# Clustered attention and two MLPs in one program: the first gate weights and one output-weight tile converted inside the unwritten attention output, and another order at both ends of the first MLP

## The chip, the cores and the metric

The program runs on one core of one Trainium2 chip. The metric is the device time of one execution in microseconds (us). Five engines work side by side, each on its own queue in order: PE (matrix multiply; its weight loads are listed as PEld), DVE (vector), ACT (activation), POOL (GpSimd) and SP, which here only issues DMAs. "SPq" is such a queue's own time. A semaphore holds an instruction until what it needs is done, and everything behind it on that engine stands too.

## The reference, cut to what matters

```python
# attention: batch 2, 8 heads, 768 rows, head width 64, 16 clusters
q_assign, k_assign = argmax(normalised q . centroids), argmax(normalised k . centroids)
scores = where(q_assign == k_assign, q @ k.T / 8, -1e9)
x = softmax(scores) @ v                      # laid out as 1536 x 512
# first MLP, weights given as float64
x = sigmoid(x @ w_gate) * (x @ w_val) @ w_out          # 512 -> 1536 -> 512
# mixture of four experts
p = domain_probs / (domain_probs.sum(-1) + 1e-9)
out = sum over e of p[:, e] * (relu(x @ w1[e]) @ w2[e])   # 512 -> 1024 -> 512
```

## The kernel before, in words

**Numbers.** PE multiplies fp32 words of reduced width, so every operand is split into a high and a low part, and a product is three matmuls (high x high, high x low, low x high). A split is one ACT copy (the high part) and one subtraction on DVE or POOL (the low part). The weights of the first MLP arrive as 64-bit words. A *conversion* of 128x512 such words has six instructions: two ACT passes in `magnitude` (Abs of the upper word, line 628, and a scaled copy of the lower word in place, line 629), three DVE steps in `bits` (clamp, shift, sign: lines 634, 635, 636) and one integer add on POOL in `rounded` (line 641).

**Attention** is 96 steps: 8 pairs of heads (4 for each batch), 2 heads, 6 row blocks of 128. Step i issues the scores S of block i+2 (line 427) and their row maximum on DVE (line 430), a third of a value product PV (lines 460, 461), six transposes T of block i (line 447), their high part on ACT (line 450) and low part pl on DVE (line 451), and the exponential of block i+2 on ACT (line 438). The preparation of later pairs and the finishing of earlier ones are cut into named pieces. `SLOT` gives each piece a step, counted from its pair's first step, and a place in that step (0 before PV, 1 after it, 2 at the end). For instance, `q0` to `k1` transpose q and k and write hiq, loq, hik and lok; `rows0` and `rows1` copy these by DMA into the operands L and R of the two heads (lines 385 to 390); `mask0` and `mask1` copy the cluster codes (lines 396, 397); `spread`, `xadd` and `xscale` scale the finished output, which lies in self.X, one tile R0 or R1 of 4 x 768 words for each batch. A pair's quarter of the tile is written by its `xscale`. All of these DMAs go through SP's queue, in the order in which they are written. hik, like hiq, is one buffer: the next pair's hik waits until `rows1` has copied the one before.

**The tail.** From step 84 `TAIL` places the first MLP's opening: `open` gives the space of the attention's preparation to the MLP's pools; `load`, `mag`, `bits`, `round` load and convert the first unit of gate weights (00, 01 are its halves) and of value weights (10, 11), `sums` forms four sums of weight quarters on POOL (line 671), `split` splits them (lines 679, 680). The program-wide dummy Sigmoid of line 617 brings ACT's table of that function.

**First MLP** (`moe1`). A product of two 2x2-blocked matrices is made with seven block products instead of eight (`seven`, matmuls at line 761): four PSUM banks, adds on DVE (lines 774 to 796), and work of others taken from a list, one entry after the first product, one after each of the next adds. `gate` runs it for one batch and 256 gate columns and ends in Sigmoids (line 832); `value` multiplies by them on DVE (line 844) and splits the result G into high (ACT, line 845) and low (POOL, line 846); `outp` multiplies by two tiles of output weights (lines 646 to 648) and adds into an accumulator (line 867; ACT, line 865, in pass 0). Pass 0 is written out; passes 1 to 5 are a loop of gate(p,0), outp(p-1,1), value(p,0), gate(p,1), outp(p,0), value(p,1). Output tiles are loaded into one buffer, rwo: tile 1 of a pass can be loaded only when POOL's rounding of tile 0 has read it. Tile 0 is converted in outp(p-1,1), tile 1 in gate(p,1), split behind it.

**Seam and mixture.** In the last value and output blocks the batch-0 operands of the mixture are summed (`ys`, POOL, line 982) and split (`ysplit`, lines 978, 979), and the first expert weights converted; `moe2` then runs `hidden` (seven products) and `outp` for 32 groups.

Of the kernel before, what the change touches and what calls it, by code (L numbers as in the profile page):

```python
# [28 lines left out]
def r2(ap):  # L29
# [11 lines left out]
    "xadd": (17, 1), "xscale": (18, 0),  # L41
# [23 lines left out]

TAIL = {
# [9 lines left out]
class Net:  # L76
# [79 lines left out]
    def probs(self):  # L156
        nc, c = self.nc, self.cpool
        self.pn = c.tile([128, B, NT, E], F32, name="pn")
        for b in range(B):
            nc.scalar.dma_start(out=self.pn[:, b], in_=self.dp[b * S:(b + 1) * S].rearrange("(p t) e -> p t e", t=NT))  # L160
# [15 lines left out]
    def prep(self, n):  # L176
# [203 lines left out]
        def rows(hh):  # L380
            def go():
# [3 lines left out]
                dma(out=L1[0:64], in_=qh)  # L385
                dma(out=R1[0:64], in_=kh)
                dma(out=R1[64:128], in_=kh)
                dma(out=L1[64:128], in_=ql)
                dma(out=L2[0:64], in_=qh)
                dma(out=R2[0:64], in_=kl)  # L390
# [145 lines left out]
    def attention(self):  # L536
# [41 lines left out]
        self.u0 = [self.unit(0, which) for which in range(2)]  # L578
        self.outers = [self.outer(f) for f in range(F1 // 128)]
        tail = {"open": self.open_weights, "outer0": self.outers[0]["load"], "outer1": lambda: self.outers[1]["load"](True)}  # L580
        for which in range(2):
            u = self.u0[which]
            tail["sums%d" % which] = lambda u=u: u["sums"](pool)
            for a in range(2):
                for name in ("load", "mag", "bits", "round"):
                    tail["%s%d%d" % (name, which, a)] = lambda u=u, a=a, name=name: u[name](a)
            for k in range(4):
                tail["split%d%d" % (which, k)] = u["split"][k]
        for name, at in TAIL.items():
            work.setdefault((LAST + at[0], at[1]), []).append(tail[name])  # L590
# [24 lines left out]
        for _, g in pvs:  # L615
            list(g)
            self.nc.scalar.activation(self.warm1, self.half[:, 0:1], AF.Sigmoid)
# [7 lines left out]
    def magnitude(self, raw, f):  # L625

        lo_w, hi_w = self.words(raw)
        self.nc.scalar.activation(f, hi_w.bitcast(F32), AF.Abs, scale=float(2.0 ** 16))
        self.nc.scalar.activation(lo_w, lo_w.bitcast(U32), AF.Copy, scale=float(2.0 ** -29))
# [56 lines left out]
    def unit(self, p, which):  # L686
# [4 lines left out]
        def load(a):  # L691
            raws[a] = self.raw.tile([128, 2, 256], I64, name="raw", tag="raw")
# [6 lines left out]
        def mag(a):  # L699
            if a == 0:  # L700
                u["c"] = self.cv.tile([128, 2, 2, 256], F32, name="cv", tag="cv")
            self.magnitude(raws[a], half(a))
# [12 lines left out]
    def outer(self, f):  # L715
        nc, t = self.nc, {}

        def load(spare=False):
            t["r"] = self.raw.tile([128, 1, 512], I64, name="raw", tag="raw") if spare else \
                self.rwo.tile([128, 1, 512], I64, name="rwo", tag="rwo")  # L720
            nc.sync.dma_start(out=t["r"][:, 0, :], in_=self.wo[f * 128:f * 128 + 128, :])

        def mag():
            t["hi"], t["lo"] = (self.wom.tile([128, 512], F32R, name=n, tag=n) for n in ("woh", "wol"))
# [458 lines left out]
```

## Time and profile before

| what | value |
|---|---|
| median of 3 runs | 1086.05 us (1085.29 to 1087.23) |
| profiled execution, its own time | 1086.53 us |
| its span, first to last instruction | 1084.7 us |
| mean granted PE clock | 0.987 of full speed |
| busy: PE, PEld | 1041.2 us (96%), 966.0 us (89%) |
| busy: DVE, POOL, ACT | 824.4 us (76%), 637.5 us (59%), 548.5 us (51%) |

Attention ends near 278 us, the first MLP near 583 us; the rest is the mixture. A timeline row gives the start in us from the span's start, the duration, engine, line, operation, output<-inputs, shapes and count, and in brackets the idle time of the engine before it with what ended that. A row of stretches gives busy us of each engine (and instructions), the granted clock of PE, the share of time in which the 16 DMA engines were busy and GB/s. A group of waits gives us in total, times, longest.

### The profile page before, as it was taken

The numbers are of one execution on the slowest core, as the hardware profiler recorded it, in microseconds if no ns is written. First come the engines' busy times: TensorE is split into PE (matmuls) and PEld (weight loads), VectorE is DVE, ScalarE is ACT, GpSimd is POOL, SyncE is SP. The second block draws the span as 40 slices with busy tenths as digits, with TensorE's granted clock in tenths as the row PEclk, the third lists the DMA queues.
The fourth block names the chain that finished last, engine by engine and source line by source line (L and its number), as shares of the span: only waits on it lengthen the run. The fifth ranks groups of instructions, "written<-read, shape, count | busy, mean of one in ns | idle before, by whom it ended". The sixth has DMA issues, their size and how long they took to land.

```text
span 1084.7 us, 16243 instructions
## 1 busy us (share of the span) xinstructions
PE 1041.2 (96%) x5813; PEld 966.0 (89%) x5813; DVE 824.4 (76%) x1407; ACT 548.5 (51%) x1156; POOL 637.5 (59%) x568
## 2 busy tenths in 40 slices
PE   6999999997889999999998999999999999999998
PEld 5899999897789999999987899889988998899887
DVE  6999899899656677767767877777678867766765
ACT  4888799888555444444434433333334433333320
POOL 7566568776758666776777644444445544444430
PEclk8999999998989999999999999999999999999999
DMA  7667766753222111222120221222122312221201
GB/s 176 138 159 172 163 151 156 161 149 108 63 66 70 60 59 59 78 78 68 52 77 21 96 75 43 78 78 76 41 79 98 107 49 78 79 69 48 78 20 59
DMA packets 86480, 95.86 MB, mean 88 GB/s; under 512 B 42720, under 2 KB 59456, under 8 KB 86400
## 3 DMA queue, kind: packets, MB, share of 16 engines
q1 hardware_dynamic: 85968, 94.77, 32.1%
q8 instruction: 46, 0.75, 0.3%
q14 instruction: 34, 0.28, 0.1%
q10 hardware_dynamic: 432, 0.06, 0.0%
HBM read 65.07 MB, written 3.19 MB: 63 GB/s over the span
## 4 chain that ended last, share of the span: by engine, by line
PE 80%; DVE 9%; POOL 3%; ACT 3%; issue 2%; DMA 2%; SPq 0%; POOLq 0%; DVEq 0%; ACTq 0%
PE ph L761 31%; PE po L1058 8%; PE po L1059 8%; PE po L1057 8%; PE T L447 5%; PE S L427 4%; PE po L648 3%; PE po L647 3%; PE po L646 2%; PE PV L460 2%; PE PV L461 2%; DVE nm L430 1%; DVE pl L451 1%; DMA R<-hik 1%; POOL co L641 1%
## 5 line engine op out<-in xcount | busy, mean ns | idle before, releaser
L1014 POOL TENSOR_TENSOR wol<-r,woh 128x512 fp32r<-128x512 f32 x62 | 80.3, 1295 | 152.9 <-ACT woh L1013 151.7
L1064 DVE SCALAR_TENSOR_TENSOR acc<-po,pn,acc 128x512 f32<-128x512 f32 (+1 forms) x181 | 129.8, 742 | 36.3 <-PE po L1059 36.3
L1059 PE MATMUL po<-woh,h2l 128*128 128x512 f32 (+1 forms) x374 | 145.7, 389 | 0.0
L1058 PE MATMUL po<-wol,h2h 128*128 128x512 f32 (+1 forms) x374 | 145.6, 389 | 0.0
L1057 PE MATMUL po<-woh,h2h 128*128 128x512 f32 (+1 forms) x374 | 145.0, 388 | 0.0
L680 POOL TENSOR_TENSOR w1l<-sf,w1h 128x512 fp32r<-128x512 f32 x88 | 113.8, 1314 | 45.7 <-ACT w1h L679 42.7
L1033 ACT ACTIVATE h2h<-ph 128x384 fp32r<-128x384 f32 x128 | 62.6, 490 | 124.2 <-PE ph L761 96.9
L761 PE MATMUL ph<-h,w1h 128*128 128x384 f32 x336 | 114.2, 340 | 4.3 <-DVE ph L782 2.0
L761 PE MATMUL ph<-h,w1l 128*128 128x384 f32 x336 | 112.8, 336 | 0.7 <-POOL w1l L680 0.7
L761 PE MATMUL ph<-l,w1h 128*128 128x384 f32 x336 | 112.7, 335 | 0.0
L451 DVE TENSOR_TENSOR pl<-T,ph 128x384 fp32r<-128x384 f32 x192 | 97.3, 548 | 14.7 <-ACT ph L450 12.7
L679 ACT ACTIVATE w1h<-sf 128x512 fp32r<-128x512 f32 x88 | 55.7, 634 | 86.1 <-DVE sf L671 68.0
L1034 DVE SCALAR_TENSOR_TENSOR h2l<-ph,h2h 128x384 fp32r<-128x384 f32 x128 | 71.0, 554 | 34.0 <-ACT h2h L1033 30.8
L450 ACT ACTIVATE ph<-T 128x384 fp32r<-128x384 f32 x192 | 84.7, 493 | 21.0 <-PE T L447 20.5
L430 DVE TENSOR_REDUCE nm<-S 128x1 f32<-128x768 f32 x96 | 91.1, 949 | 2.0 <-PE S L427 1.0
L427 PE MATMUL S<-R,L 80*128 80x384 f32 (+1 forms) x384 | 91.4, 360 | 0.7 <-ACT P L438 0.7
L447 PE MATMUL T<-ident,P 128*128 128x128 f32 x576 | 83.3, 279 | 7.5 <-DVE pl L451 3.7
L438 ACT ACTIVATE P<-S,nm 128x768 f32<-128x768 f32 x96 | 87.7, 913 | 3.6 <-DVE nm L430 3.6
L680 POOL TENSOR_TENSOR w1l<-r,w1h 128x512 fp32r<-128x512 f32 x64 | 67.0, 1048 | 37.4 <-ACT w1h L679 37.4
L1059 PEld LDWEIGHTS po<-woh,h2l 128*128 128x128 f32 x374 | 70.2, 188 | 14.5
L1057 PEld LDWEIGHTS po<-woh,h2h 128*128 128x128 f32 x374 | 70.2, 188 | 13.9
L1058 PEld LDWEIGHTS po<-wol,h2h 128*128 128x128 f32 x374 | 70.2, 188 | 13.9
(264 smaller groups left out, 2851.7 us busy)
## 6 DMA issues: line engine op xcount, KB each, us to landing
r<-in_moe_w_dram SPq DMA_DIRECT2D x64, 512.0 KB, 3.6
L<-hiq SPq DMA_DIRECT2D x32, 192.0 KB, 4.6
R<-hik SPq DMA_DIRECT2D x32, 192.0 KB, 5.1
raw<-in_moe_w_gate_dram SPq DMA_DIRECT2D x12, 512.0 KB, 3.8
raw<-in_moe_w_val_dram SPq DMA_DIRECT2D x12, 512.0 KB, 3.8
rwo<-in_moe_w_out_dram SPq DMA_DIRECT2D x11, 512.0 KB, 3.5
nq<-in_q_dram SPq DMA_DIRECT2D x16, 192.0 KB, 4.5
nk<-in_k_dram SPq DMA_DIRECT2D x16, 192.0 KB, 3.6
```

What stands on the lines that cost most here:

```text
L427: nc.tensor.matmul(ps[:, a, 0:384], l[0:k, c], r[0:k, a * 384:a * 384 + 384], start=l is L1, stop=l is L2)
L430: nc.vector.tensor_reduce(nm, ps[:, :, 0:384], axis=AX.XY, op=ALU.max, negate=True)
L438: nc.scalar.activation(r2(pt), ps[:, :, 0:384], AF.Exp, bias=nm, scale=1.0, accum_out=P["sums"][:, i:i + 1])
L447: nc.tensor.transpose(ps[:, j, :], pt[:, c:c + 128], self.ident)
L450: nc.scalar.activation(hi, ps, AF.Copy)
L451: nc.vector.tensor_tensor(lo, ps, hi.bitcast(F32), op=ALU.subtract)
L680: nc.gpsimd.tensor_tensor(lo[:, sl], x, hi[:, sl].bitcast(F32), op=ALU.subtract)
L761: nc.tensor.matmul(ps, x[:, a, j], y[:, j], start=first and j == 0 and k == 0, stop=j == 1 and k == 2, skip_group_check=not first)
L1057: nc.tensor.matmul(ps, Hh[:, f, c], wh[:, dc], start=f == 0, stop=False)
L1058: nc.tensor.matmul(ps, Hh[:, f, c], wl[:, dc], start=False, stop=False)
L1059: nc.tensor.matmul(ps, Hl[:, f, c], wh[:, dc], start=False, stop=f == 1)
L1064: nc.vector.scalar_tensor_tensor(a, ps, pe, a, op0=ALU.mult, op1=ALU.add)
```

## The change

The first unit of gate weights and output tile 0 are converted in steps 12 to 52 (`SOON`) inside self.X, in parts that no pair has written yet; the tail keeps the value unit's conversion, earlier and spread over steps, and the splits of the gate unit move to steps 85 and 86. `t1`, the first operand sum of batch 1, is put at step 86, and the table load at step 93. `rows1` comes half a step earlier, with the key rows first for the second head; `xadd` and `xscale` half a step later. The domain probabilities are loaded by SP's queue instead of ACT's and normalised in value(0,1). In `moe1` the conversion of output tile 1 moves to the first gate block in pass 0 and into value(p,0) in the loop; at the end the operand splits and the conversion of pair 1 get another order. `spare1`, `temp1` and `room` are the former inner functions of `moe1`.

```diff
 SLOT
-"rows1": (-7, 0)   "xadd": (17, 1), "xscale": (18, 0)
+"rows1": (-8, 1)   "xadd": (18, 0), "xscale": (18, 2)
+SOON = {
+    "load00": (12, 2), "load01": (13, 2), "abs00": (15, 2), "low00": (24, 2), "bits00": (24, 25, 27), "round00": (28, 2),
+    "abs01": (27, 2), "low01": (36, 2), "bits01": (36, 37, 39), "round01": (40, 2),
+    "loado": (29, 2), "abso": (39, 2), "lowo": (48, 2), "bitso": (48, 49, 51), "roundo": (52, 2),
+}
 TAIL = {
-    "open": (-12, 0), "load00": (-12, 0), "load01": (-12, 0),
-    "mag00": (-10, 2), "bits00": (-9, 1), "round00": (-9, 1), "load10": (-9, 1),
-    "mag01": (-9, 2), "bits01": (-8, 1), "round01": (-8, 1), "load11": (-8, 1), "sums0": (-7, 2),
-    "split00": (-7, 2), "split01": (-6, 2), "mag10": (-5, 2), "split02": (-5, 2), "bits10": (-4, 1), "round10": (-4, 1),
-    "split03": (-4, 2), "outer1": (-4, 2), "mag11": (-4, 2), "bits11": (-3, 1), "round11": (-3, 1), "outer0": (-6, 2),
-    "sums1": (-2, 2),
+    "open": (-12, 0), "load10": (-12, 0), "load11": (-12, 0), "sums0": (-12, 2), "outer1": (-11, 2),
+    "split00": (-11, 2), "split01": (-11, 2), "split02": (-10, 2), "split03": (-10, 2), "t1": (-10, 2),
+    "mag10": (-9, 2), "bits10": (-8, -8, -7), "round10": (-7, 2), "mag11": (-7, 2), "bits11": (-6, -6, -5),
+    "round11": (-5, 2), "sums1": (-3, 2), "table": (-3, 2),
 }
 def probs
-            nc.scalar.dma_start(out=self.pn[:, b], ...
+            nc.sync.dma_start(out=self.pn[:, b], ...
+    def normalise(self):
 def rows
+                parts = [(L1[0:64], qh), (R1[0:64], kh), (R1[64:128], kh), (L1[64:128], ql), (L2[0:64], qh),
+                         (R2[0:64], kl)]
+                for o, x in [parts[i] for i in ((0, 1, 2, 3, 4, 5) if hh == 0 or first else (1, 2, 0, 4, 5, 3))]:
+                    dma(out=o, in_=x)
 def attention
-        self.u0 = [self.unit(0, which) for which in range(2)]
+        R0, R1 = (x.rearrange("p a s -> p (a s)") for x in self.X)
+        raws = [r.bitcast(I64)... for r in (R1[:, 0:1024], R0[:, 2048:3072])]
+        self.u0 = [self.unit(0, 0, raws, R1[:, 1536:2560]...), self.unit(0, 1)]
+        o0 = self.outer(0, raws[0], R1[:, 2560:3072])
...
         for _, g in pvs:
             list(g)
-            self.nc.scalar.activation(self.warm1, self.half[:, 0:1], AF.Sigmoid)
 def moe1
-        c, d = conv(o0), conv(o1)
-        sums["t1"]()
+        d = conv(o1)
-        gate(0, 0, [[lambda: split0(6, Q), vs[0]], [lambda: split0(2, V), vs[1]], c[0] + [vs[2]], c[1] + [vs[3]],
-                    c[2], c[3] + c[4], [xadd, xscale, o0["split"]]])
+        gate(0, 0, [[lambda: split0(6, Q), vs[0]], [lambda: split0(2, V), vs[1]], [vs[2]] + d[0], d[1] + [vs[3]],
+                    d[2], d[3] + d[4] + [o0["split"]], [xadd, xscale]])
-        value(0, 0, [[sums["t2"]], [go[0]] + d[0], d[1] + [sums["t3"]], d[2], d[3] + d[4], [sums["t4"], o1["split"]],
-                     [lambda: split(0, V), go[1]]])
+        value(0, 0, [[o1["split"], go[0]], [sums["t2"]], [go[1]], [], [], [], [sums["t3"], lambda: split(0, V), sums["t4"]]])
-        value(0, 1, [load(U[1][1])] + [[go] for go in U[1][0]["split"]])
+        value(0, 1, [load(U[1][1])] + [[go] for go in U[1][0]["split"]] + [[self.normalise]])
             o1["load"]()
-            value(p, 0, [[], [o0["split"]]])
             e = conv(o1)
+            value(p, 0, [[], [o0["split"]], [], e[0], e[1], e[2], e[3] + e[4]])
-                gate(p, 1, [e[0], e[1], e[2], e[3] + e[4], [o1["split"]] + c[0], c[1] + c[2], c[3] + c[4]])
+                gate(p, 1, [[o1["split"]], c[0], c[1], c[2], c[3], c[4]])
-        gate(NP - 1, 1, [e[0], e[1], e[2], e[3] + e[4], [o1["split"]]])
+        gate(NP - 1, 1, [[o1["split"]]])
-        value(NP - 1, 1, [[ys[0], out[1], lambda: self.load_out2(1)], [lambda: ysplit(0, V), ys[1]], [lambda: ysplit(1, V)], []])
-        outp(NP - 1, 1, [[ys[2], lambda: ysplit(4, V)], [ys[3]], [lambda: ysplit(5, V)], [lambda: ysplit(3, V)],
-                         [lambda: ysplit(6, Q)], [], [lambda: ysplit(2, Q)], [cin[0], cin[1]]], soon=True)
-        self.first_in = cin[2:]
+        value(NP - 1, 1, [[ys[0], out[1], lambda: self.load_out2(1)], [lambda: ysplit(0, V), ys[1]], [ys[2]], [], [], [],
+                          [cin[0], lambda: ysplit(4, V)]])
+        outp(NP - 1, 1, [[ys[3], lambda: ysplit(5, V)], [cin[1]], [lambda: ysplit(3, V)], [cin[2]],
+                         [lambda: ysplit(1, V)], [cin[3]], [lambda: ysplit(6, Q)], [lambda: ysplit(2, V), cin[4]]], soon=True)
+        self.first_in = []
```

In `unit` and `outer` a place that is given is used for the raw words and the result instead of a tile of the pools; `mag` can issue its two ACT passes apart; output tile 1 of pass 0 is loaded into rwo instead of a buffer of raw; the high and low tiles of an output tile are taken in `split` instead of in `mag`.

## Rows read from the trace of the kernel before

**Rows 1.** Stretches: start:end, length, busy us of each engine, PE clock, DMA share.
```profile
88.30:122.30 34.00, 31.95 (x209) 29.97 (x207) 30.06 (x53) 26.84 (x65) 23.58 (x20) 0.95 0.64 147
241.70:278.40 36.70, 31.27 (x177) 28.43 (x176) 30.00 (x48) 29.37 (x67) 23.55 (x21) 0.86 0.43 121
278.40:313.10 34.70, 27.48 (x129) 24.92 (x128) 23.76 (x29) 19.57 (x38) 24.20 (x17) 0.90 0.15 46
393.85:441.55 47.70, 46.82 (x266) 45.60 (x265) 35.04 (x64) 21.63 (x42) 33.42 (x33) 1.00 0.21 67
```

**Rows 2.** Timeline of PE in the attention tail (steps 85, 86, 93 and 95).
```profile
243.76 0.81 PE L447 MATMUL T<-ident,P 128*128 128x128 f32 x6
245.82 0.82 PE L447 MATMUL T<-ident,P 128*128 128x128 f32 x6
...
266.70 0.90 PE L447 MATMUL T<-ident,P 128*128 128x128 f32 x3 [3.44 <-ACT ph L450]
...
272.27 1.48 PE L447 MATMUL T<-ident,P 128*128 128x128 f32 x6
```

**Rows 3.** Source lines of the conversion: count, ns min/median/max, first and last start.
```profile
L634 DVE TENSOR_SCALAR cv<-cv x24: 414/890/1295, 248.7 to 527.0; 128x512 f32<-128x512 f32 x24
...
L635 DVE TENSOR_SCALAR cv<-cv x24: 414/427/1419, 249.2 to 527.4; 128x512 int32<-128x512 int32 x24
...
L636 DVE SCALAR_TENSOR_TENSOR cv<-raw,cv x24: 678/682/1649, 249.6 to 529.2; 128x512 int32<-128x512 int32 x24
...
L628 ACT ACTIVATE cv<-raw x24: 649/670/738, 248.0 to 524.7; 128x512 f32<-128x512 f32 x24
```

**Rows 4.** Timeline of ACT behind the last transposes.
```profile
276.11 1.28 ACT L617 ACT_TABLE_LOAD   x1
277.40 0.20 ACT L617 ACTIVATE warm<-half 128x1 f32<-128x1 f32 x1
```

**Rows 5.** Waits of PE in the MLP's start: us, times, longest.
```profile
PE po L647 <- POOL G L846: 2.8, 2, 2.0
```

**Rows 6.** Timeline of DVE, PE and ACT in the middle of attention.
```profile
107.47 0.20 DVE L163 TENSOR_REDUCE pns<-pn 128x12 f32<-128x48 f32 x1 [0.45 <-DMA pn<-in_moe_domain_probs_dram]
...
111.16 1.36 PE L447 MATMUL T<-ident,P 128*128 128x128 f32 x6 [1.80 <-DVE pl L451]
...
199.41 0.49 ACT L259 ACTIVATE hik<-T 128x384 fp32r<-128x384 f32 x1 [1.78 <-DMA R<-hik]
...
74.15 0.49 ACT L259 ACTIVATE hik<-T 128x384 fp32r<-128x384 f32 x1 [0.67 <-DMA R<-hik]
```

**Rows 7.** Stretches in the middle of attention, columns as in rows 1.
```profile
66.00:76.00 10.00, 9.54 (x67) 8.82 (x66) 8.75 (x17) 7.27 (x18) 4.37 (x3) 1.00 0.94 214
111.70:115.00 3.30, 3.30 (x13) 3.21 (x13) 3.08 (x5) 2.16 (x6) 2.91 (x6) 0.50 0.31 75
```

**Rows 8.** Timeline of PE and POOL in loop pass 2 (output product; rounding of tile 0).
```profile
410.58 0.44 PE L648 MATMUL po<-G,wol 128*128 128x384 f32 x1 [0.75 <-POOL wol L737]
...
396.53 1.32 POOL L641 TENSOR_TENSOR co<-co,rwo 128x512 int32<-128x512 int32 x1 [0.63 <-DVE co L636]
```

**Rows 9.** Tile rwo: its loads from issue to landing.
```profile
DMA to landing us min/median/max: 3.4/3.5/3.5
```

**Rows 10.** Chain of waits where a value block meets the gate block: start, us, what.
```profile
401.17 0.56 DVE ph L796
401.73 0.47 DVE sg L844
...
402.24 1.32 PE ph L761 x6
```

**Rows 11.** Waits of PE at the seam to the mixture: us, times, longest.
```profile
PE ph L761 <- DVE ph L782: 2.7, 2, 1.5
...
PE ph L761 <- POOL w1l L680: 0.7, 1, 0.7
```

**Rows 12.** Timeline of DVE at the seam.
```profile
566.67 2.13 DVE L979 TENSOR_TENSOR Y<-acc,Y 128x768 fp32r<-128x768 f32 x1
```

More of the change, by code (lines that the diff above doesn't have):

```diff
@@ L584, in attention @@
             for a in range(2):
-                for name in ("load", "mag", "bits", "round"):
+                for name in ("load", "mag", "round"):
                     tail["%s%d%d" % (name, which, a)] = lambda u=u, a=a, name=name: u[name](a)
+                tail["bits%d%d" % (which, a)] = lambda steps, u=u, a=a: u["bits"](a, steps)
             for k in range(4):
                 tail["split%d%d" % (which, k)] = u["split"][k]
-        for name, at in TAIL.items():
-            work.setdefault((LAST + at[0], at[1]), []).append(tail[name])
+        for names, gos, base in ((SOON, soon, 0), (TAIL, tail, LAST)):
+            for name, at in names.items():
+                if name[:4] == "bits":
+                    for k in range(3):
+                        work.setdefault((base + at[k], 1), []).append(lambda go=gos[name], k=k: go((k,)))
+                else:
+                    work.setdefault((base + at[0], at[1]), []).append(gos[name])
         def side(i, pos):
@@ L684, in left_operands, with unit @@
                    split(slice(5, 7), lambda: t["sf"][:, 2:4]), split(2, lambda: t["r"][:, 1, :, 128:256])]
-    def unit(self, p, which):
+    def unit(self, p, which, place=None, result=None):
         src = (self.wg, self.wv)[which]
@@ L691, in load @@
         def load(a):
-            raws[a] = self.raw.tile([128, 2, 256], I64, name="raw", tag="raw")
+            raws[a] = place[a] if place else self.raw.tile([128, 2, 256], I64, name="raw", tag="raw")
             self.nc.sync.dma_start(out=raws[a], in_=src[a * 256:a * 256 + 256, p * 256:p * 256 + 256]
@@ L697, in half, with mag @@
             return u["c"][:, a].rearrange("p k f -> p (k f)")
[L699 to L702, printed above, removed]
+        def mag(a, steps=(0, 1)):
+            if "c" not in u:
+                u["c"] = result if place else self.cv.tile([128, 2, 2, 256], F32, name="cv", tag="cv")
+            self.magnitude(raws[a], half(a), steps)
         def bits(a, steps=range(3)):
@@ L713, in unit, with outer, load, mag @@
         return u
-    def outer(self, f):
+    def outer(self, f, place=None, result=None):
         nc, t = self.nc, {}
-        def load(spare=False):
-            t["r"] = self.raw.tile([128, 1, 512], I64, name="raw", tag="raw") if spare else \
-                self.rwo.tile([128, 1, 512], I64, name="rwo", tag="rwo")
+        def load():
+            t["r"] = self.rwo.tile([128, 1, 512], I64, name="rwo", tag="rwo") if place is None else \
+                place.rearrange("p k f -> p (k f)").unsqueeze(1)
             nc.sync.dma_start(out=t["r"][:, 0, :], in_=self.wo[f * 128:f * 128 + 128, :])
-        def mag():
-            t["hi"], t["lo"] = (self.wom.tile([128, 512], F32R, name=n, tag=n) for n in ("woh", "wol"))
-            t["f"] = self.co.tile([128, 512], F32, name="co", tag="co")
-            self.magnitude(t["r"], t["f"])
+        def mag(steps=(0, 1)):
+            if "f" not in t:
+                t["f"] = self.co.tile([128, 512], F32, name="co", tag="co") if place is None else result
+            self.magnitude(t["r"], t["f"], steps)
         def bits(steps=range(3)):
@@ L735, in split @@
         def split():
+            t["hi"], t["lo"] = (self.wom.tile([128, 512], F32R, name=n, tag=n) for n in ("woh", "wol"))
             nc.scalar.activation(t["hi"], t["f"], AF.Copy)
@@ L807, in moe1 @@
         gs, sgs = {}, {}
-        def room(pool, t, dt=F32R):
-            return pool.tile([128, 2, HB], dt, name=t, tag=t)
-        def spare(o):
-            if o == 2:
-                return room(self.xsp, "rb"), room(self.xp, "tA")
-            if o == 6:
-                return room(self.xsp, "A"), room(self.xsp, "W")
-            return room(self.op, "g%d" % o), room(self.op, "k%d" % o)
-        def temp(o):
-            return room(self.cv, "cv", F32) if o > 4 else room(self.xp, "tA" if o == 4 else "tB", F32)
-        sums, split = self.right_operands(1, spare, temp, nc.gpsimd)
+        room = self.room
+        sums, split = self.late
         split0 = self.split0[1]
```

46 lines of the change are left out of this document (33 added, 13 removed), and 2 rows, old and new, of the table SLOT.

## The prediction

> **What bounds the kernel now.** On the page PE is the busiest engine in nearly every slice, so time can only come from stretches where it stands or runs at its lower clock. A table of stretches shows where: a pass of the first MLP's loop has PE busy 46.82 of 47.70 us at full clock, the last twelve steps of attention 31.27 of 36.70 and the first blocks of the MLP 27.48 of 34.70, at 0.86 and 0.90 of the clock [rows 1]. At the lower level (1.2 of 2.4 GHz) a microsecond does half the work, so the attention tail lost 5.4 us standing and 36.7 x 0.14 = 5.1 to the clock, the MLP's start 7.2 and 3.5. After that I read the timeline, the waits and the chain of waits inside each stretch [rows 2 to 12]: the reader is to see which instruction ended each hole.
>
> **The attention tail.** A step is 2.06 us from transposes to transposes where nothing stands, as the first two of [rows 2] show; the next nine take 26.45 us, 7.9 too many. The largest hole is 3.44 us. It ends on ACT's copy of T, but behind it stands DVE with a conversion: one half of 512 words is three DVE instructions of 0.41, 0.41 and 0.68 us alone, and 1.29, 1.42 and 1.65 at their longest (1.5 against 4.4 us a half) [rows 3], the long ones while POOL runs. The change takes two halves of four out of the tail. Two remain, beside POOL's splits, so they may cost 4.4 each. ACT loses two halves of 2 x 0.67 [rows 3] and gains the table load, 1.28 us and its dummy of 0.20 [rows 4], which stood where ACT was idle and now stands ahead of the last copies of T. The splits of the gate weights come earlier, together with POOL's four sums; ACT waits for those sums, with the copies of T queued behind. Bounds: 9 us gained (the hole, its clock and half a microsecond) to 2 (both halves at the long price, the clock falls anyway). I take **6**: the halves no longer stand behind one another, but ACT is fuller at steps 85 to 89.
>
> For the table load there is a rule. Here the load took 1.28 us and the next ACT instruction began 0.01 us after it [rows 4]. The Trainium skill, "ScalarE: Activation LUTs", section "What ACT_TABLE_LOAD costs", states a load plus a drain, about 2.66 us together; by that the tail would gain 1.2 us less. The trace shows no such drain here.
>
> **The MLP's start.** PE waits 2.8 us for POOL's low halves of G [rows 5], while POOL rounds and splits tile 1 of the output weights among them. After the change tile 0 comes converted and tile 1 takes its place in the first gate block: that block has the same DVE and POOL work as now, but the value block loses a round and its three DVE steps (1.5 to 4.4 us [rows 3]). The new wait: DVE's xscale writes over tile 0's result, so it stands until POOL has split that, with the value block's adds behind it on DVE. POOL comes to that split about when it does now, so I count 1 us. Bounds: 3 (the wait for G alone) to 10.7 (all that this stretch lost). I take **7**.
>
> **The middle of attention.** Gains: the four small DVE steps on the domain probabilities begin at 107.47, ahead of a row maximum; PE then stands 1.80 us [rows 6] and runs 3.3 us at the lower clock [rows 7], 1.8 + 1.65 = 3.45. They move to the end of the value block of pass 0, where DVE has room [rows 1]. Copying the key rows first lets ACT overwrite hik one copy earlier: ten copies of 192 KB fill a 10 us stretch at a DMA share of 0.94 [rows 7], 0.94 us each, off a wait of 1.78 us [rows 6]; I count 0.9. The half step by which rows1 moves passes nothing on SP's queue: 0.
>
> Costs: two 512 KB loads now stand on SP's queue at steps 12 and 13, ahead of the attention copies and rows1 of that round, in the stretch just named, which is full. A loop pass holds six such loads at a share of 0.21 of 47.70 us [rows 1], 1.67 us each. So key rows land 3.3 - 0.94 = 2.4 us later, and ACT, which already waits 0.67 us for them there [rows 6], waits 3.1; behind it stand U and the next PV. With the lower clock after it (1.65) that is 4.0. Bounds: 0, if the loads pass beside the copies, to 6. I take 4.0, since copies in this stretch are late already. Nine DVE steps join three pairs: 4.6 us cheap to 13 dear, against 3.9 us free in 34 by the first of [rows 1], in steps where POOL mostly idles. 0 to 5; I take 1.5. ACT's six passes (0.67 each, 7.2 of 34 us free) and POOL's three rounds (1.3 each, 10.4 free) I cost at nothing; without that room each would cost its own length once. The same goes for xadd and xscale half a step later, the third load at step 29 and the probabilities' two issues on SP, all of which stand after rows1. Sum: 3.45 + 0.9 - 4.0 - 1.5 = **-1.2**.
>
> **The loop.** In each of five passes the output product waits 0.75 us for POOL's split of tile 1, and restarts slowly (0.44 us for that one product) [rows 8]: 1.0 together. Its conversion now comes in the value block, and that loss goes: 5 x 1.0 = 5. But its load waits for the one buffer, which POOL's rounding of tile 0 frees at 397.85 [rows 8]; it lands 3.4 us on [rows 9], at 401.3, just where the value block's products end (401.14). The conversion is written after the first eviction, so ACT stands for the load, then 0.67 us of Abs; DVE's first bit step (0.4) stands until then, and the two adds and the eviction that free the bank for the next gate block's second product stand behind it, with the second bit step (0.4) between. Today that chain is add 0.56, multiply 0.47, PE, with no slack [rows 10]. New: 401.3 + 0.7 + 0.4 + 0.5 + 0.4 + 0.5 + 0.5 = 404.3 instead of 402.2, a hole of 2.1 us, or 3.2 if the second bit step meets POOL (1.42). Net 5 x 2.1 - 5 = 5.5, to 11; if nobody is held it is the gain of 5. I take **-6**, near the cheap end, as POOL is idle when the first step runs.
>
> **The seam to the mixture.** PE waits 2.7 us in two holes for one add on DVE and 0.7 for the weights of pair 1 [rows 11]. A split of 2.13 us stands ahead of that add on DVE [rows 12] and leaves; pair 1's sums and splits move ahead of the seam. In exchange POOL has three sums instead of two ahead of G, so the wait for G may grow by one sum, 1.9 us. Bounds 0 to 4.5 (the two waits and the slow restarts behind them); I take **3**.
>
> **Sum**: 6 + 7 - 1.2 - 6 + 3 = 8.8 us. The profiled execution took 1086.53 us around a span of 1084.7; it stands 0.5 above the median of 1086.05. 1086.5 - 8.8 = 1077.7, in terms of the median **1077**. What this kernel can tell from no change is 0.2%, 2.2 us.
>
> **Rivals.**
> 1. *Both ends gain and the loop pays part back* (forecast, 0.46): 1077, with 1071 to 1084 of its own.
> 2. *The loop gains too* (0.17): the late conversion holds nobody, because it doesn't stand where the diff writes it or its load lands 2 us sooner. For it: POOL's rounding that frees the buffer waits on DVE steps that meet POOL today, and could come sooner; against: in the loop of the kernel before, DVE's order is the written one. 5 instead of -6: 1066.
> 3. *Slower* (0.21): the hole of the loop is at its long end, 3.2 us, and the lower clock follows each one. For it: holes of 1.80 and 3.44 us idle [rows 2, 6] were followed by it [rows 1, 7]; against: 2.1 us is nearer to the shorter of them, and each pass alike would have to meet POOL. 5 x (3.2 + 1.65 - 1.0) = 19 lost instead of 6: 1090. It decides from a net loss of 3.4 us a pass, where the other 14.8 us are used up by 2.2 more.
> 4. *The loss only moves* (0.16): in the middle the nine DVE steps meet POOL at the long price (-3.5 more), and the tail, full on ACT, gains 2 instead of 6: 1085, no change.
>
> **Chances.** Faster: all of 2, nearly all of 1 and little of 4, 0.65. Within 0.2%: most of 4 and a rest of 1 and 3, 0.14. Slower: most of 3, some of 4, 0.21. The range goes from rival 2 with its tail near the upper bound, 1064, to rival 3, 1090.
>
> **What the profile after would show.** Right: no hole over 2 us between steps 86 and 95 and no lower clock there; the wait of the output product for G under 1 us; no DVE work on pn in attention; a wait of ACT for R<-hik near 3 us at step 18; in each pass a new hole of 2 to 3 us at the gate's second product ended by DVE's multiply, and none for wol. Wrong: no such hole (rival 2), the lower clock in every pass (rival 3), or holes at steps 24 to 52 that end on DVE's pl (rival 4).

## The result, and the profile after

The changed kernel took **1097.06 us** (median of 4 runs, 1092.86 to 1100.0) against 1085.67 for the kernel before: ratio 1.0100, 95% interval 1.0062 to 1.0138. It is slower by 1%, where 0.8% faster was forecast. The profiled execution (1095.45 us) has a span of 1093.7 us against 1084.7, so 9.0 us are to be found. One of the twelve executions of start_order (run 8 below) took 2062.55 us where the others took 1079.9 to 1086.0; its ratio leaves that one out.

The page of the changed kernel, span, busiest engines and granted clock:

```profile
span 1093.7 us, 16218 instructions
...
PE 1043.5 (95%) x5813; PEld 971.4 (89%) x5813; DVE 821.6 (75%) x1408; ACT 549.1 (50%) x1155; POOL 638.9 (58%) x567
...
PEclk8999999999999999999999999999999999999999
```

Little there tells that 9 us were lost: PE has 2.3 us more busy time and 6.7 us more idle time. Stretches tell more. In the next view the first row is the attention tail, from step 84 to attention's last product, where the forecast cut it too [rows 1]; the second and third are the MLP's start, up to gate(0,1) and up to the loop; then come two loop passes, the second and the third, each from one first product of `outp(p,0)` to the next (columns as in [rows 1]):

```profile
243.20:279.90 36.70, 31.25 (x186) 28.09 (x184) 28.55 (x43) 27.34 (x63) 21.87 (x20) 0.95 0.27 82
279.90:311.70 31.80, 25.93 (x119) 22.54 (x118) 21.59 (x26) 18.01 (x34) 22.42 (x16) 0.89 0.12 39
311.70:345.50 33.80, 31.02 (x176) 30.09 (x175) 23.15 (x38) 20.86 (x44) 24.71 (x24) 1.00 0.22 63
363.60:413.90 50.30, 48.04 (x265) 47.19 (x264) 34.38 (x63) 21.76 (x42) 33.73 (x33) 0.97 0.21 63
413.90:464.20 50.30, 46.57 (x265) 45.62 (x265) 34.41 (x63) 21.76 (x42) 33.77 (x32) 1.00 0.21 63
```

Cut at the same instructions, the kernel before gives the lengths of the second column:

| stretch | before | after | gain | forecast |
|---|---|---|---|---|
| start of attention to its step 84 | 241.7 | 243.2 | -1.5 | -1.2 |
| step 84 to attention's last product | 36.7 | 36.7 | 0.0 | +6 |
| MLP's start, from there to gate(0,1) | 34.6 | 31.8 | +2.8 | +7 |
| gate(0,1) to value(1,0) | 33.0 | 33.8 | -0.8 | 0 |
| loop, value(1,0) to value(5,1) | 215.4 | 227.3 | -11.8 | -6 |
| value(5,1) to the end | 523.3 | 520.9 | +2.3 | +3 |

The sum is -9.0. (Of the first row 1.0 us lies ahead of attention's second step, where the changed code is the same; other profiles have -0.2 to +0.9 there. loop_only, run 2 below, has the attention of the kernel before and reaches step 84 0.9 us later than it, so a difference of 1 us in this row says little.) The MLP's first products stand between attention's last ones, 14 matmuls of them ahead of attention's last product where 5 stood before, so the second and third rows run into each other; their sum, 2.8 of 13, is firmer than either. A loop pass is 50.3 us instead of 47.7 [rows 1]. Where PE stood, by what ended it (engine, line waited for: us in total, times, longest):

```profile
PE ph L788 <- DVE sg L872: 11.3, 6, 2.2
PE T L452 <- DVE pl L456: 8.4, 6, 2.7
PE ph L788 <- DVE ph L809: 5.6, 5, 1.5
...
PE po L673 <- POOL G L874: 3.2, 2, 2.5
...
PE ph L788 <- DVE u L801: 2.6, 1, 2.6
```

L872 is the multiply of `value` (L844 before), and five of its six waits are the loop's. The wait for `wol` [rows 8] is gone. But L809, the add of `gate`, is new in the loop: 4.4 of the 5.6 us lie in passes 1, 3 and 4. The timeline of pass 2, POOL, ACT, DVE and PE in order of time, and last a row of pass 3:

```profile
397.92 1.31 POOL L667 TENSOR_TENSOR co<-co,rwo 128x512 int32<-128x512 int32 x1 [0.63 <-DVE co L662]
...
402.90 0.66 ACT L653 ACTIVATE co<-rwo 128x512 f32<-128x512 f32 x1 [1.13 <-POOL G L874]
...
403.60 0.43 DVE L660 TENSOR_SCALAR co<-co 128x512 f32<-128x512 f32 x1 [1.93 <-ACT co L653]
403.94 0.56 DVE L818 TENSOR_TENSOR ph<-u,ph 128x384 f32<-128x384 f32 x1
404.40 0.42 DVE L661 TENSOR_SCALAR co<-co 128x512 int32<-128x512 int32 x1
404.74 0.55 DVE L823 TENSOR_TENSOR ph<-u,ph 128x384 f32<-128x384 f32 x1
405.20 1.01 DVE L872 TENSOR_TENSOR sg<-sg,ph 128x384 f32<-128x384 f32 x2
...
405.81 0.44 PE L788 MATMUL ph<-g,w1h 128*128 128x384 f32 x1 [2.20 <-DVE sg L872]
...
410.64 1.29 POOL L764 TENSOR_TENSOR wol<-co,woh 128x512 fp32r<-128x512 f32 x1 [0.74 <-ACT woh L763]
...
411.15 1.07 DVE L660 TENSOR_SCALAR cv<-cv 128x512 f32<-128x512 f32 x1 [1.37 <-ACT cv L653]
412.14 0.55 DVE L809 TENSOR_TENSOR ph<-u,ph 128x384 f32<-128x384 f32 x1
...
463.08 0.44 PE L788 MATMUL ph<-rb,w1h 128*128 128x384 f32 x1 [1.50 <-DVE ph L809]
```

The upper part is the forecast's chain, step for step: POOL's rounding ends at 399.23 and frees the one buffer, the load is issued at 399.25, ACT's Abs starts at 402.90, one of DVE's steps stands ahead of the first add (L818) and one between the two, PE stands 2.20 us (forecast 2.1). In the five passes the hole is 1.42, 2.20, 2.16, 1.99 and 2.04 us. The row of the Abs names POOL's G, which ended at the same moment, but Abs doesn't read G; in the other four passes, where it starts 3.4 to 3.6 us behind the issue, the row names the load. The lower part wasn't forecast: the first step of the *gate* conversion (L660 on `cv`) begins while POOL splits tile 1, takes 1.07 us instead of 0.43, and the add L809 stands behind it. In pass 2 PE doesn't wait for that add, as it ran at half clock between 406.8 and 409.9 us and came later; in pass 3, at full clock, the same order makes it stand 1.50 us.

The attention tail, DVE and POOL:

```profile
254.19 2.14 DVE L660 TENSOR_SCALAR cv<-cv 128x512 f32<-128x512 f32 x1
254.22 1.83 POOL L525 TENSOR_TENSOR tB<-R 128x768 f32<-128x768 f32 x1
...
260.69 1.82 POOL L507 TENSOR_TENSOR A<-A,W 128x768 f32<-128x768 f32 x1
...
260.90 1.90 DVE L660 TENSOR_SCALAR cv<-cv 128x512 f32<-128x512 f32 x1
262.59 1.87 POOL L510 TENSOR_TENSOR R<-A,rb 128x768 f32<-128x768 f32 x1
...
262.83 1.91 DVE L661 TENSOR_SCALAR cv<-cv 128x512 int32<-128x512 int32 x1
...
265.26 0.55 PE L452 MATMUL T<-ident,P 128*128 128x128 f32 x3 [2.72 <-DVE pl L456]
```

Each long step of DVE ends 0.28 or 0.29 us after the POOL instruction beside it (256.33 behind 256.05, 262.80 behind 262.51, 264.74 behind 264.46), whenever that began. So it isn't slowed, it stands until POOL is done. All twelve profiles say the same: each of their 421 clamps and shifts of 0.5 us or more ends 0.27 to 0.30 us after a POOL instruction. The other 443 take 0.41 to 0.45 us, 95 of them although a POOL instruction starts while they run. What counts is that POOL is at work when DVE's step comes, and at what: 45 of the short ones ran while POOL formed the small root `rn` (128x24 words, 4.2 us). (The first row begins 0.03 us ahead of L525, but behind the start of POOL's subtraction before it, which ends at 254.25.) The Trainium skill, "SBUF — State Buffer", section "Who interferes with whom", states this as a rule: DVE's copies and tensor_scalar in their faster modes need a pair of ports that POOL uses too, and one instruction holds it to its end. The three rows agree in that each step ends behind POOL's; the 45 short steps beside the root don't fit the words "to its end", and there the measurement decides. All three POOL instructions were put there by the change: L525 is the operand sum `t1` (moved to step 86), L507 and L510 are `xadd` and `xscale` of the seventh pair (moved by half a step).

The middle of attention and the MLP's start, ACT, POOL and DVE:

```profile
72.62 0.66 ACT L653 ACTIVATE R<-R 128x512 f32<-128x512 f32 x1 [4.50 <-DMA R<-in_moe_w_gate_dram]
...
79.27 0.49 ACT L266 ACTIVATE hik<-T 128x384 fp32r<-128x384 f32 x1 [1.87 <-DMA L<-hiq]
...
290.28 2.03 POOL L667 TENSOR_TENSOR co<-co,rwo 128x512 int32<-128x512 int32 x1
292.26 1.30 POOL L764 TENSOR_TENSOR wol<-R,woh 128x512 fp32r<-128x512 f32 x1
...
293.60 2.00 DVE L510 TENSOR_TENSOR R<-A,rb 128x768 f32<-128x768 f32 x1 [2.46 <-POOL wol L764]
295.52 0.54 DVE L801 TENSOR_TENSOR u<-m,ph 128x384 f32<-128x384 f32 x1
...
326.74 0.79 DVE L171 TENSOR_SCALAR pns<-pns 128x12 f32<-128x12 f32 x1
```

In the kernel before, `xscale` followed `xadd` at once:

```profile
289.76 1.95 DVE L505 TENSOR_TENSOR R<-A,rb 128x768 f32<-128x768 f32 x1
```

The rows show three things: two waits of ACT where one of [rows 6] was; `xscale` (L510) behind the split of tile 0, which stands behind the rounding of tile 1 on POOL, with the add L801 behind it (PE stands 2.59 us); and the normalisation, whose small steps meet POOL and hold the multiply (PE stands 1.51 us).

### The profile page after: what moved, and what is told of

Its sections match the earlier page's. It is cut to its first block, busy times and chain, and to the rows that moved or that the text cites. A ratio compares the mean times of both kernels' runs of the same rounds, so it can differ in the third digit from the quotient of the medians.

```text
span 1093.7 us, 16218 instructions
## 1 busy us (share of the span) xinstructions
PE 1043.5 (95%) x5813; PEld 971.4 (89%) x5813; DVE 821.6 (75%) x1408; ACT 549.1 (50%) x1155; POOL 638.9 (58%) x567
## 4 chain that ended last, share of the span: by engine, by line
PE 69%; POOL 11%; DVE 8%; issue 6%; DMA 3%; ACT 2%; SPq 0%; POOLq 0%; DVEq 0%; ACTq 0%
PE ph L788 27%; PE po L1085 8%; PE po L1086 8%; PE po L1084 8%; PE T L452 4%; PE S L432 4%; POOL w1l L706 2%; PE PV L465 2%; PE PV L466 2%; PE po L673 2%; PE po L674 1%; PE po L672 1%; DMA rwo<-in_moe_w_out_dram 1%; DMA L<-hiq 1%; POOL sf L697 1%
## 5 line engine op out<-in xcount | busy, mean ns | idle before, releaser
L1061 DVE SCALAR_TENSOR_TENSOR h2l<-ph,h2h 128x384 fp32r<-128x384 f32 x128 | 70.9, 554 | 34.0 <-ACT h2h L1060 30.8
L452 PEld LDWEIGHTS T<-ident,P 128*128 128x128 f32 x576 | 67.7, 142 | 17.5 <-DVE pl L456 12.0
```

The source lines that it names most:

```text
L452: nc.tensor.transpose(ps[:, j, :], pt[:, c:c + 128], self.ident)
```

## The experiments

Theory: the loss is the loop's, 2.4 us a pass, from two places where DVE is held; the other parts gain little, as DVE meets POOL in the tail and the start and the two loads fill the DMA queue in the middle. The rivals are named with each run. Every run was timed against the kernel before on the same chip; that kernel's median was 1085.7 to 1086.5 us each time. A run is also set beside the changed kernel, whose four executions took 1092.9 to 1100.0 us.

**1. loop_back: the loop undone in the changed kernel.**

```diff
-            value(p, 0, [[], [o0["split"]], [], e[0], e[1], e[2], e[3] + e[4]])
+            value(p, 0, [[], [o0["split"]]])
-                gate(p, 1, [[o1["split"]], c[0], c[1], c[2], c[3], c[4]])
+                gate(p, 1, [e[0], e[1], e[2], e[3] + e[4], [o1["split"]] + c[0], c[1] + c[2], c[3] + c[4]])
...
```

(The last pass's gate is put back in the same way.)

> The changed kernel with the loop part alone undone: the conversion of output tile 1 stands again in gate(p,1) of passes 1 to 5, and the gate conversions behind it at their old places. Theory (the loop part costs about 2.4 us a pass, as the profile of the changed kernel shows it: 3.6 to 3.9 us up to the output product, 1.25 won back there): the loop period returns to 47.70 us, the holes of 2.0 to 2.2 us before the second product of gate(p,1) and those of 1.5 us behind DVE's add L809 are gone, and the kernel is 11.8 us faster than the changed one: 1085 us by the medians, about the kernel before. Rival (the loop part only shows a loss that stands elsewhere, as a late operand that the lower clock then makes dear): less than 6 us come back, 1091 or more.

Measured: 1085.52 us, ratio 1.000 (0.9986 to 1.0014). A pass:

```profile
407.30:455.00 47.70, 46.82 (x266) 45.60 (x265) 35.03 (x62) 21.59 (x43) 33.41 (x32) 1.00 0.22 67
```

The theory holds: the loop alone makes the loss. It says a second thing, too: all the other parts together, for which 14.8 us were forecast, are worth 0 within 1.5 us by the ratio's interval.

**2. loop_only: the loop's edit in the kernel before** (the two lines above the other way round, with the high and low tiles taken in `split`).

> The kernel before with the loop part alone: tile 1 converted in value(p,0), the gate conversions one entry on in gate(p,1), high and low tiles taken at the split. Theory: 5 passes at 2.4 us, 11.8 us slower than the kernel before, 1097.5 us; in each pass a hole of 2.0 to 2.2 us before the second product of gate(p,1), and behind it either a second hole of 1.5 us on DVE's add or a stretch at half clock. Rival: on its own it costs half or less, up to 1091, and the rest came with the other parts of the change.

Measured: 1099.56 us, ratio 1.0118 (1.0099 to 1.0136), 12.8 us slower by the ratio. Two passes:

```profile
364.80:415.30 50.50, 46.67 (x267) 45.71 (x266) 34.52 (x63) 21.74 (x42) 33.87 (x33) 1.00 0.21 63
415.30:467.50 52.20, 48.78 (x265) 48.14 (x264) 34.82 (x63) 21.97 (x43) 34.52 (x33) 0.93 0.21 61
```

The rival falls: without the other parts the loop costs about as much as with them (12.8 us here, 11.5 between the changed kernel and loop_back). The second of these passes has half clock behind its hole, and a longer hole, 3.36 us: there ACT's Abs starts 4.8 us behind the load's issue (455.75 behind 450.96) and not 3.4 to 3.65. So the hole is as long as that load is late.

**3. loop_late: the same conversion in value(p,0), two entries later.**

```diff
-            value(p, 0, [[], [o0["split"]], [], e[0], e[1], e[2], e[3] + e[4]])
+            value(p, 0, [[], [o0["split"]], [], [], [], e[0], e[1], e[2], e[3] + e[4]])
-                gate(p, 1, [[o1["split"]], c[0], c[1], c[2], c[3], c[4]])
+                gate(p, 1, [[o1["split"]], [], c[0], [], c[1], c[2], c[3] + c[4]])
```

> The changed kernel with tile 1 still converted in value(p,0), but two entries later in the lists (ACT's Abs behind the second add, DVE's three steps behind the block's last two multiplies), and with the gate conversions of gate(p,1) two entries later, clear of POOL's split of tile 1. Theory (the loss is the order on ACT and DVE: the Abs waits for the one buffer's load, and DVE's first steps stand ahead of the adds; the second hole is DVE's clamp beside POOL's split): both holes go, the output product's wait for wol stays away, and a pass is 1.2 us shorter than in the kernel before, 46.5 us: 5 x (2.4 + 1.2) = 18 us faster than the changed kernel, 1079. Rival (the loss is the load itself, or the length of the conversion, wherever it is written): the hole only moves to the output product or to the next block, and the kernel stays at 1091 or more.

Measured: 1080.96 us, ratio 0.9948 (0.993 to 0.9965): 16 us less than the changed kernel. A pass:

```profile
409.50:456.10 46.60, 46.47 (x265) 45.68 (x265) 36.10 (x63) 21.50 (x43) 33.59 (x33) 1.00 0.23 68
```

PE has no hole of 0.2 us in the five passes. The rival falls. At this place neither the single buffer nor the conversion's length costs anything; what costs is that DVE's steps stand ahead of adds which PE waits for. The idea of the change was sound, and its place in the lists was wrong by two entries.

**4. c_late: only the gate conversions later** (the second of the two edits above).

> The changed kernel with the gate conversions of gate(p,1) two entries later, clear of POOL's split of tile 1; tile 1 is converted in value(p,0) as in the changed kernel. Theory (two holes with causes of their own: 2.1 us by the late load, 1.5 us by DVE's clamp beside POOL's split; half clock is granted only in single passes): the second hole of 1.5 us goes in every pass, the first stays, and a pass costs 2.1 - 1.2 = 0.9 us more than in the kernel before: 5 x 1.5 = 7.5 us faster than the changed kernel, 1090. Rival (each first hole is followed by half clock, which costs 1.7 us and in the changed kernel took the place of the second hole in passes 2 and 5): every pass keeps 2.4 us of loss, half clock behind each hole, and the time stays at 1096 to 1098.

Measured: 1091.27 us, ratio 1.0047 (1.0033 to 1.006): 5.8 us less than the changed kernel, between the two. Two passes:

```profile
412.20:462.20 50.00, 47.85 (x266) 47.21 (x265) 34.39 (x63) 21.62 (x43) 33.83 (x32) 0.97 0.20 64
462.20:510.60 48.40, 46.27 (x265) 45.63 (x265) 33.58 (x61) 21.09 (x42) 33.86 (x32) 1.00 0.20 61
```

The holes of 1.5 us are gone in all passes and the first holes stay (1.42 to 2.15 us). Both were partly right: a hole of 2.1 us costs 48.4 - 47.7 = 0.7 us net where the clock stays up and 2.3 where it falls. In the changed kernel, passes 2 and 5 had half clock and no second hole, passes 1, 3 and 4 the second hole and full clock; pass 2 is as long as pass 3.

**5. abs_late: ACT's first Abs later, the loads in place.**

```diff
-    "load00": (12, 2), "load01": (13, 2), "abs00": (15, 2),
+    "load00": (12, 2), "load01": (13, 2), "abs00": (20, 2),
```

> The changed kernel with ACT's first Abs of gate half 00 put at step 20 instead of 15, the loads where they are (steps 12 and 13). Theory A (ACT stood 4.5 us for the load itself, with the copy of T behind it): the stall of 2.5 us before the transposes of step 17 goes, ACT's wait for R<-hik at step 18 stays or grows a little, so steps 16 to 18 lose 1.2 to 2.5 us against the kernel before instead of 4.1: 2 to 3 us faster than the changed kernel, 1094.5. Theory B (my forecast: the two loads delay the copies of the key rows, and ACT waits for these): 4 us are lost there still, and the time does not move: 1097.

Measured: 1097.73 us, ratio 1.0107 (1.0087 to 1.0126), as the changed kernel. Wait of ACT between 60 and 90 us:

```profile
ACT hik L266 <- DMA R<-hik: 6.9, 1, 6.9
```

Theory B holds, and at a higher price than forecast: without the wait for the load, ACT stands 6.9 us for the key rows (0.67 in [rows 6]), which go behind the loads in SP's queue. In the changed kernel the Abs only took part of that wait on itself. From steps 16 to 20 this run lost 8.7 us; six profiles with the loads at this place lost 3.5 to 7.1 there.

**6. load_late: the loads behind the copies.**

```diff
-    "load00": (12, 2), "load01": (13, 2), "abs00": (15, 2),
+    "load00": (18, 2), "load01": (19, 2), "abs00": (23, 2),
```

> The changed kernel with the two loads of the gate weights at steps 18 and 19, behind rows1 on SP's queue, and the first Abs at step 23. Both theories of the step 16 to 18 loss say that it goes whole: 4.1 us less than the changed kernel, 1093 us, no hole over 0.7 us between steps 14 and 20. If a later queue (the value load, onehot's copies) takes the loss over, 1095 to 1097, with the hole at a later step.

Measured: 1094.32 us, ratio 1.0074 (1.0057 to 1.0091), 2.7 us less than the changed kernel. The same wait of ACT:

```profile
ACT hik L266 <- DMA R<-hik: 0.5, 1, 0.5
```

The two intervals overlap, so the medians alone don't show the 2.7; the profile does: the loss between steps 16 and 20 is gone whole. In this profile 2.0 us of it came back around step 45, where the same kind of copies came late (ACT waited 1.95 us for R<-hik at 137.31). Whether the copies come late because they stand behind the loads in the queue, or because both share the DMA engines, no run here separates.

**7. tail_clear: POOL's long instructions away from the tail's conversions** (on loop_back).

```diff
-    ... "split03": (-10, 2), "t1": (-10, 2),
-    ... "mag11": (-7, 2), "bits11": (-6, -6, -5), "round11": (-5, 2), "sums1": (-3, 2),
+    ... "split03": (-10, 2),
+    ... "mag11": (-6, 2), "bits11": (-4, -4, -3), "round11": (-3, 2), "sums1": (-2, 2),
         d = conv(o1)
+        sums["t1"]()
```

> The kernel of loop_back (the changed one with the loop undone) with POOL's long instructions taken from beside the two conversions in the attention tail: the operand sum t1 goes back to the head of gate(0,0), and the second half's conversion comes one to two steps later, behind xadd and xscale. Theory (DVE's clamp and shift stand until the POOL instruction that runs beside them is over: 2.14, 1.90 and 1.91 us instead of 0.41, and the transposes wait for pl behind them): the holes of 1.65 and 2.73 us in the tail go, and with the half clock that follows; the tail is 4 to 6 us shorter than in loop_back, 1080 to 1081.5 us, and clamp and shift take 0.4 to 0.9 us. Rival (ACT or the queue of the row maxima bounds the tail, and the conversions only fill waits): under 1.5 us are won, with the holes at other steps, and DVE's clamp as long as before.

Measured: 1082.89 us, ratio 0.9968 (0.9954 to 0.9982), 2.6 us less than loop_back. Its tail (35.8 us in loop_back), and DVE and POOL in it:

```profile
242.20:275.20 33.00, 30.38 (x184) 27.65 (x183) 24.30 (x43) 27.30 (x63) 21.87 (x21) 0.95 0.30 92
```

```profile
246.65 1.84 POOL L525 TENSOR_TENSOR tB<-R 128x768 f32<-128x768 f32 x1
...
254.92 0.43 DVE L659 TENSOR_SCALAR cv<-cv 128x512 f32<-128x512 f32 x1
255.39 0.43 DVE L660 TENSOR_SCALAR cv<-cv 128x512 int32<-128x512 int32 x1
...
264.56 0.41 DVE L659 TENSOR_SCALAR cv<-cv 128x512 f32<-128x512 f32 x1
```

Clamp and shift take 0.41 to 0.43 us, the holes of 1.65 and 2.73 us are gone, and the tail is 2.8 us shorter, which the medians bear out: the cause holds, at less than the 4 to 6 us that were expected. (The MLP's first product comes 4.6 us sooner, but 29 of attention's matmuls now stand behind it and not 19.) `t1` ran at 246.65, between the sums of the gate weights and not at the head of `gate(0,0)`, where it is written, and a new hole of 1.89 us at 250.86 follows.

**8. start_order: tile 1 rounded behind the split of tile 0, the probabilities normalised in outp(1,0)** (on loop_back).

```diff
-        gate(0, 0, [..., d[2], d[3] + d[4] + [o0["split"]], [xadd, xscale]])
-        value(0, 0, [[o1["split"], go[0]], ...
-        value(0, 1, [load(U[1][1])] + ... + [[self.normalise]])
+        gate(0, 0, [..., d[2], d[3] + [o0["split"]], [xadd, xscale]])
+        value(0, 0, [d[4] + [o1["split"], go[0]], ...
+        value(0, 1, [load(U[1][1])] + ...)
-                outp(p, 0, [..., [split[0]], [], [split[1]]])
+                outp(p, 0, [..., [split[0]], [self.normalise] if p == 1 else [], [split[1]]])
```

> The kernel of loop_back with POOL's rounding of output tile 1 put behind the split of tile 0 (it is written first in value(0,0)), so that DVE's xscale waits less, and with the domain probabilities normalised in outp(1,0) instead of value(0,1). Theory: xscale now waits 2.46 us for the split, which stands behind a rounding of 2.03 us; without that it starts 1.3 to 2 us sooner, and the hole of 2.6 us in value(0,0) shrinks to 0.6 to 1.3; the hole of 1.51 us before gate(0,1)'s successor, which DVE's four small steps make (0.79 and 0.70 us beside POOL), goes and does not come back in outp(1,0): together 2.5 to 3.5 us, 1082 to 1083. Rival (POOL is the bound of this stretch, so the rounding is late for the split of tile 1 and G instead): the sum of the holes between 285 and 313 us stays, and only the 1.5 us of the probabilities are won, 1084.

Measured: 1082.96 us, ratio 0.9972 (0.9959 to 0.9984), 2.6 us less than loop_back. DVE's xscale:

```profile
294.49 2.05 DVE L510 TENSOR_TENSOR R<-A,rb 128x768 f32<-128x768 f32 x1 [1.19 <-POOL wol L764]
```

The theory holds: xscale waits 1.19 us instead of 2.46, PE's hole behind it is 1.37 instead of 2.60, and the one of 1.51 us is gone. xscale still takes 2.05 us (xadd, of the same shape, 1.02), now with POOL's rounding beside it. The start up to gate(0,1) takes 29.2 us, from there to value(1,0) 33.0.

**9. all_ends: loop_late, load_late and start_order together, with the tail and the seam cleared in the same way.**

```diff
+    tail: "round10": (-7, 2), "t1": (-7, 2), "mag11": (-5, 2), "bits11": (-3, -3, -2), "round11": (-2, 2), "sums1": (-1, 2)
-    seam: value(NP - 1, 1, [..., [lambda: ysplit(0, V), ys[1]], [ys[2]], ...
+    seam: value(NP - 1, 1, [..., [lambda: ysplit(0, V), ys[1]], [], ...
+          outp(NP - 1, 1, [[ys[2]], [ys[3], cin[1]], [lambda: ysplit(5, V)], [lambda: ysplit(3, V), cin[2]], ...
```

> A version built from the findings: the changed kernel with loop_late's order in the loop, load_late's loads in the middle of attention, start_order's rounding and normalisation, and two changes by the same reading of DVE and POOL: in the tail the operand sum t1 stands behind the first half's rounding and the second half's conversion two to three steps later, so that no clamp or shift has a POOL instruction beside it; at the seam the third operand sum on POOL stands behind the products of the last value block, so that G's low half waits for one sum less. Theory: loop 6 us less than the kernel before, tail 4 to 6, start with the normalisation 4, middle 2 to 3, seam 3 to 4: 19 to 23 us together, 1063 to 1067; clamp and shift near 0.43 us throughout the tail. Rival (the tail's and the seam's losses only move to the next POOL instruction, as t1's did in tail_clear): those two give 3 us together, 1070 to 1073.

Measured: **1068.23 us**, ratio 0.9833 (0.9821 to 0.9846): 18 us faster than the kernel before and 29 faster than the changed one, between the two expectations. Its span, its tail and a pass:

```profile
span 1066.4 us, 16224 instructions
```

```profile
241.40:272.20 30.80, 29.34 (x184) 26.35 (x183) 23.75 (x43) 27.06 (x63) 21.94 (x21) 1.00 0.32 95
...
396.10:442.60 46.50, 46.37 (x267) 45.73 (x266) 35.34 (x63) 21.63 (x43) 34.02 (x33) 1.00 0.22 68
```

Tail and loop came as expected (5.9 and 6 us less than before). At the seam the wait for G shrank to 1.13 us, but a hole of 2.88 us came behind it: accumulator adds stand on DVE until 559.79, behind a sum of weight quarters of 2.06 us, with the moved sum beside it on POOL, and an operand split of 2.57 us.

**10. seam_back: all_ends with the changed kernel's seam.**

> The kernel of all_ends with the seam as the changed kernel has it (the third operand sum on POOL again in the last value block). Theory (in all_ends the wait for G shrank, but a hole of 2.88 us with half clock came behind it, where four accumulator adds stand on DVE behind an operand split that waits for the late sum): the wait for G is 2.45 us again instead of 1.13, the hole of 2.88 us is 0.9 or less, and the stretch from the last output block to the end is 513.6 us instead of 515.2: 1 to 2 us faster than all_ends, 1066 to 1067. Rival (the two holes are the same wait, seen at two places): no difference, 1068.

Measured: 1069.51 us, ratio 0.984 (0.9819 to 0.986). The wait for G is the long one again and the other hole is gone:

```profile
PE po L673 <- POOL G L874: 3.6, 2, 2.5
```

The last stretch is 513.8 us instead of 515.2, yet the median isn't lower. The profile shows where the 1.4 us went: between steps 42 and 48 of attention, where both kernels are the same code, seam_back lost 3.6 us more, with a hole of 2.78 us behind a wait of ACT for late copies. How often the copies come so late no run here tells, so the seam's worth stays open; all_ends and seam_back are one result.

## Why the prediction was wrong

1. **The loop: right mechanism, size wrong.** The hole was forecast at 2.1 us and is 1.99 to 2.20 in four passes and 1.42 in the first; the gain was forecast at 1.0 a pass and is 1.1 to 1.2 (loop_late, all_ends). The step that failed: "Net 5 x 2.1 - 5 = 5.5", taken as -6, with the hole as the only price. A pass costs 2.6 us net, 2.4 in the mean of the five, because a second price was left out in each: the gate conversion's clamp, which the new list puts beside POOL's split of tile 1 (1.5 us), or, where the clock fell, half clock (1.6 by c_late). The rival of the slower side named the half clock, but in every pass and with a longer hole; it gave 19 us where 12 were lost. That DVE's step could meet POOL was counted for the tile's conversion only, not for the list that moved up behind it.
2. **The tail: the step "I take **6**: the halves no longer stand behind one another" failed.** The forecast knew that a half may cost 4.4 us beside POOL and held it for a price of splits. The change itself moves three POOL instructions of 1.82 to 1.87 us beside the two halves that stay, and both clamp and shift stand until they end. The tail takes 36.7 us as before, under the lower bound of 2 gained, with holes of 1.66 and 2.72 us where none over 2 was to be. tail_clear takes 33.0 and all_ends 30.8: the 6 were there to be had. (The dearer price that was weighed for the table load should have been 1.4 us and not 1.2, as the dummy's 0.20 runs in either case; it wasn't paid: in the changed kernel the load took 1.28 us again, and the next ACT instruction began 0.01 us behind it.)
3. **The MLP's start: "POOL comes to that split about when it does now, so I count 1 us" failed.** POOL comes to it behind tile 1's rounding of 2.03 us; xscale then waits 2.46 and takes 2.00. 2.8 us were gained where 7 were forecast, under the lower bound of 3, and the normalisation, costed at nothing "where DVE has room", took 0.8 of that back behind gate(0,1). start_order shows 2.6 us for these two. With both undone this stretch is 5.4 us shorter than before (34.6 to 29.2); the other 1.6 of the 7 came in no run, and why stays open. The wait for G fell as forecast (0.74 us).
4. **The middle: the sum is right, -1.5 for -1.2, in part by luck.** Steps 16 to 20 lost 4.1 us in the profiled execution (4.0 forecast), in two waits instead of one, but 3.5 to 7.1 in six profiles with the loads at this place. The normalisation's leaving gained 3.2 (3.45 forecast). Steps 52 to 72 gained 2.4, put down to the key rows copied first (0.9 forecast); a hole of 1.58 us that ended on ACT is gone there. The nine DVE steps, costed at 1.5, show no loss over 0.7 between steps 24 and 52. Of 1.9 us lost between steps 72 and 84, 1.0 is a hole at step 75, where DVE's `rn` waits for POOL's root; I put that down to the half step of xadd and xscale, which was costed at nothing. And 1.0 us of the sum lies ahead of all changed code.
5. **The seam: right**, +2.3 of 3; the wait for G grew by 1.66 us (0.80 to 2.46) where one sum, 1.9, was forecast.

Together: the tail and the MLP's start, with the normalisation, fell short by 11 us, the loop cost 5.8 more. Had only the loop been wrong, the kernel would still have been faster by the forecast's own sum.

## What to carry to other kernels

When steps move in a list, write down for every short DVE step which POOL instruction is running when it comes at its *new* place, and for every add that a matmul waits for, what now stands ahead of it. A move by one or two entries changed this loop from 12 us slower to 6 faster. And price a load not only by its own landing: the copies issued behind it came late here (a wait of ACT went from 0.67 to 6.9 us), and putting the load behind those that someone waits for took that loss away.

## What the runs showed of the hardware

- A clamp or shift of 128x512 words takes 0.41 to 0.45 us alone, and beside a POOL instruction of 1.83 us it ends 0.28 us after that one: 1.90 to 2.14 us. The profile shows it as busy all that time. A second such step right behind it can meet POOL's next instruction. A POOL instruction that starts while the step runs doesn't hold it (95 times in the twelve profiles), nor does POOL's root of 128x24 words (45 times).
- Holes alike are not followed alike: in one execution of the changed kernel the granted clock fell to half (1.2 of 2.4 GHz) after holes of 2.20 and 2.04 us and stayed at full after 2.16 and 1.99. In loop_back holes of 1.65 and 2.73 us in the tail left the tail's clock at 1.00, in the changed kernel the same two left it at 0.95. A fall cost 1.6 us a pass (c_late, 50.0 against 48.4).
- A 512 KB load lands 3.4 to 3.5 us after its issue in the loop of the kernel before [rows 9]; the two behind attention's copies took 7.0 us (median of the two) in the changed kernel and 9.7 in abs_late.
